# When ScalarE scales the blocks of w1 and w2: tied behind its own last cast, and queued after older blocks' casts

## The chip, the cores and the metric

The kernel runs on one core of a Trainium2 chip. The core has five engines that work side by side, each with a queue of its own in a fixed order: TensorE (PE in the profile), VectorE (DVE), ScalarE (ACT), GpSimd (POOL) and SyncE (SP), which here only issues transfers. The metric is the device time of one execution in microseconds, lower being better; times are compared as medians of several runs.

## The reference

```python
x = attention(q, k, v)            # B=4, H=8, S=576, D=64, causal window of 64 -> (2304, 512)
a = x @ w1; b = x @ w2            # 512 -> 1024 each
h = a * b @ w3                    # (a * b) @ w3, 1024 -> 1024
y = h @ w_out                     # 1024 -> 512
g = np.maximum(0.01 * (y @ w_in), y @ w_in)    # 512 -> 2048
out = g @ w_out2                  # 2048 -> 512
```

All weights arrive as float64 words, read as pairs of 32-bit integers.

## The kernel before

**Products.** Each fp32 product is made of three matmuls on operands split in a high and a low part (`mm3`, lines 77 to 79): high by high, high by low, low by high. The third one, line 79, is the first that needs the low part of the weights.

**Stages.** First the fold w3 @ w_out is computed (`w3_tr`, `w3_mm`, 16 steps), with the attention of the first 384 tokens between its steps. Then five chunks of tokens follow. A chunk has eight column steps f = 0 to 7: `ab_step(c, f, 0)` multiplies by w1, `ab_step(c, f, 1)` by w2, ScalarE and VectorE form their product and split it (lines 669 to 676), and `y_step` multiplies it by the fold. The `y_step` of f comes one step late, so that of f=0 stands after the products of f=1. A product's PSUM bank comes free when line 669 (first product) or line 674 (second) has read it; there are two such banks. Later stages (w_in, w_out2) follow and end the kernel.

**Conversion of weights.** Weights are converted from float64 in units. A unit is loaded by SyncE (`load_unit`, line 382), *scaled* by ScalarE with two activations (lines 417 and 391), *shifted* by VectorE (line 438), given its *sign* bits by VectorE (line 396), and *finished* by `store`: ScalarE casts the high part (line 332), and for w1 and w2 GpSimd subtracts to get the low part (line 333). `advance` moves up to four units on by one step each, and `until` calls it until a unit is finished.

**The eight units of w1 and w2.** They come last in this phase; here they are called B0 to B7: B0 is the first 256 columns of w1, B1 those of w2, B2 and B3 the next 256 columns of each, and so on. Steps f=0 and f=1 need B0 and B1, f=2 and f=3 need B2 and B3, and so on. B0, B2, B4, B6 share one place for raw words and one for the converted ones, B1, B3, B5, B7 the other. So the load of B2 can start when the sign step of B0 has read its words, and the shift of B2 can start when GpSimd has read the converted B0.

**What sets the order.** A scheduler decides where in each engine's queue an instruction stands, from priorities and its own estimate of times; the queue is then fixed. `tc.issue_after(x)` forces the instructions of a block to stand behind x on the same engine; it adds no wait on another engine. The first two units of w1 and w2 are loaded well ahead, during the fold; in the code, B0's scaling is written in the call `until(W12, PHASE_B)` after the fold's last step, and the scheduler moves it up.

Of the kernel before, what the change touches and what calls it, by code (L numbers as in the profile page):

```python
# [8 lines left out]
F32 = mybir.dt.float32  # L9
# [12 lines left out]
def tile_kernel(ctx: ExitStack, tc: tile.TileContext, q, k, v, w1, w2, w3, w_out, w_in, w_out2, out):  # L22
# [44 lines left out]
    act, dve, pool, pe, sp = nc.scalar, nc.vector, nc.gpsimd, nc.tensor, nc.sync  # L67

    def f32(ap):
        return ap.bitcast(F32)  # L70

    def first():

        return tc.high_priority(offset=3000)

    def mm3(ps, lh, ll, rh, rl, first, last, more=False):
        pe.matmul(ps, lhsT=lh, rhs=rh, start=first, stop=False, skip_group_check=more)  # L77
        pe.matmul(ps, lhsT=lh, rhs=rl, start=False, stop=False, skip_group_check=more)  # L78
        return pe.matmul(ps, lhsT=ll, rhs=rh, start=False, stop=last, skip_group_check=more).ins  # L79
# [243 lines left out]
    def cols2(t):  # L323
        return t.rearrange("p s (k m) -> p s k m", m=2 * P)
# [26 lines left out]
    def part_of(kind, dims, dt=F32):  # L351

        n = 1
        for d in dims:
            n *= d
        if words_in is not None:
            return words_in.tile([P] + list(dims), dt, name=kind, tag=kind, bufs=RAW)
        i = n_of[kind] % RAW
        n_of[kind] += 1
        x = {"raw": raw_all, "f": f_all}[kind][:, i].bitcast(dt)[:, 0:n]  # L360
        return shaped(x, dims)

    def feed():

        while n_of["load"] < n_of["cap"] and n_of["bits"] >= units[n_of["load"]]["after"]:
            load_unit()

    def load_unit():
        i = n_of["load"]
        u = units[i]  # L370
        n_of["load"] += 1
        u["raw"] = u["at"]() if u["at"] else part_of("raw", [UC], I64)
        with ExitStack() as how:
            if i >= PHASE_B:
                if i > PHASE_B + RAW:
                    how.enter_context(tc.issue_after(pss["store"]))
            else:
                how.enter_context(first())
            if "load" in pss:
                how.enter_context(tc.issue_after(pss["load"]))  # L380
            d = shaped(u["raw"], u["src"].shape[1:]) if len(u["src"].shape) == 3 else u["raw"]
            x = sp.dma_start(d, u["src"]).ins
        if i < PHASE_B:
            pss["load"] = x
            start_loads(i)
        else:
            pss.pop("load", None)

    def low_bits(raw, n=UC):

        act.activation(out=raw.bitcast(I32).rearrange("p (m two) -> p m two", two=2)[:, :, 0],
                       in_=raw.bitcast(U8).rearrange("p (m e) -> p m e", e=8)[:, :, 3],
                       func=AF.Copy, scale=1.0 / 32, bias=-31.0 / 64)

    def sign(f, hi):
        dve.scalar_tensor_tensor(out=f, in0=hi, scalar=-0x80000000, in1=f, op0=ALU.bitwise_and, op1=ALU.bitwise_or)

    def f_free(i):

        if i >= PHASE_B:  # L400
            return True
        a, n = units[i]["f_at"]
        for j in range(i):
            b, m = units[j]["f_at"]
            if a < b + m and b < a + n and (n_of["fin"] <= j or not units[j]["free"]()):
                return False
        return True

    def advance(stop):

        now = dict(n_of)
        if now["scale"] < min(stop, now["load"]):
            u = units[now["scale"]]
            w = u["raw"].bitcast(I32).rearrange("p (m two) -> p m two", two=2)
            u["lo"], u["hi"] = w[:, :, 0], w[:, :, 1]
            if now["scale"] < PHASE_B:
                act.mul(u["hi"].bitcast(F32), u["hi"].bitcast(F32), 2.0 ** -112)
                low_bits(u["raw"])
            else:
                u["f"] = part_of("f", [UC])  # L420
                with tc.issue_after(pss["copy"]):
                    act.mul(u["f"], u["hi"].bitcast(F32), 2.0 ** -112)
            n_of["scale"] += 1
        if now["fin"] < now["bits"]:
            u = units[now["fin"]]
            u["fin"](u["f"])
            n_of["fin"] += 1
        d = now["bits"] < now["shift"]
        if d:
            u = units[now["bits"]]  # L430
            f = u["f"].bitcast(I32)
            sign(f, u["hi"])
        if now["shift"] < now["scale"] and f_free(now["shift"]):
            u2 = units[now["shift"]]
            if now["shift"] < PHASE_B:
                i, n = u2["f_at"]
                u2["f"] = f_all[:, i:i + n].rearrange("p n m -> p (n m)")
                dve.scalar_tensor_tensor(out=u2["f"].bitcast(I32), in0=u2["hi"], scalar=3, in1=u2["lo"],
                                         op0=ALU.logical_shift_left, op1=ALU.bitwise_or)
            else:  # L440
                g = u2["f"].bitcast(I32)
                dve.tensor_scalar(g, g, 3, 0x7FFFFFF8, op0=ALU.logical_shift_left, op1=ALU.bitwise_and)
            n_of["shift"] += 1
        if d:
            if now["bits"] >= PHASE_B:
                dve.scalar_tensor_tensor(out=f, in0=u["lo"], scalar=29, in1=f, op0=ALU.logical_shift_right, op1=ALU.bitwise_or)
            n_of["bits"] += 1
            feed()

    def until(n, stop):  # L450
        while n_of["fin"] < n:
            was = dict(n_of)
            advance(stop)
            assert n_of != was
# [9 lines left out]
    pss = {}  # L464

    def w3_tr(f):
        t = p0.tile([P, 2, 4, P], F32R, name="w3T", tag="w3T", bufs=2)
        ps = ps_ab.tile([P, 4, P], F32, name="ab", tag="ab")
        for i in range(4):
            pe.transpose(ps[:, i, :], f[:, i], ident)  # L470
        both = t.rearrange("p s i k -> p s (i k)")
        act.copy(both[:, 0], ps.rearrange("p i k -> p (i k)"))
        pss["dve"] = dve.tensor_tensor(out=both[:, 1], in0=ps.rearrange("p i k -> p (i k)"), in1=f32(both[:, 0]),
                                       op=ALU.subtract).ins
        w3T.append(t)
# [48 lines left out]
    for gi in range(2):  # L524
        for l in range(2 if gi == 0 else 0, KF, 2):
            i = len(units)
            unit(w3[4 * P * gi:4 * P * gi + 4 * P, P * l:P * l + 2 * P].rearrange("(k p) m -> p k m", p=P), wide_w3(gi, l),
                 ("w3", gi, l), PLACES[i % 4], AFTER.get(i, i - 3), (2 * (i % 2), 2))
            if gi == 0:
                i = len(units)  # L530
                unit(w_out[P * l:P * l + 2 * P, :].rearrange("(k p) m -> p k m", p=P), store(("wo", l // 2), None),
                     ("wo", l), PLACES[i % 4], AFTER.get(i, i - 3), (2 * (i % 2), 2))
    W12 = len(units)
    for p in range(KD):
        for w, name in ((w1, "w1"), (w2, "w2")):
            i = len(units)
            unit(w[:, 2 * P * p:2 * P * p + 2 * P].rearrange("(k p) m -> p k m", p=P), store((name, p), None), (name, p),
                 PLACES[2 + i % 2], i - 3 if i < W12 + 2 else i - 1, (2 * (i % 2), 2))
    PHASE_B = len(units)
# [117 lines left out]
    def ab_step(c, f, j):  # L657
        n = W * CHUNKS[c][1]
        p, e = divmod(f, 2)
        ps = ps_ab.tile([P, 4, P], F32, name="ab", tag="ab").rearrange("p t k -> p (t k)")[:, 0:n]  # L660
        w = cols2(slots[("w1", "w2")[j], p])
        for kk in range(KD):
            x = xt[c, kk]
            ws = slice(P * e, P * e + P)
            pss["last"] = mm3(ps, w[:, 0, kk, ws], w[:, 1, kk, ws], x[:, 0, 0:n], x[:, 1, 0:n], kk == 0, kk == KD - 1)
        if j == 0:
            pss["a"] = gp.tile([P, CW], F32, name="a32", tag="a32", bufs=1)[:, 0:n]
            with first():
                pss["copy"] = act.copy(pss["a"], ps).ins
            return  # L670
        p32 = gp.tile([P, CW], F32, name="p32", tag="p32", bufs=1)[:, 0:n]
        t = gp.tile([P, 2, CW], F32R, name="ab", tag="ab", bufs=2)[:, :, 0:n]
        with first():
            dve.tensor_tensor(out=p32, in0=ps, in1=pss["a"], op=ALU.mult)  # L674
            act.copy(t[:, 0], p32)
            pss["dve"] = dve.tensor_tensor(out=t[:, 1], in0=p32, in1=f32(t[:, 0]), op=ALU.subtract).ins  # L676
        ab[f] = t

# [192 lines left out]
    for c in range(NC):  # L871
        for i in range(3 * KF):
            f, part = divmod(i, 3)
            if c == 0:
                if part == 0:
                    until(max(last[n, f // 2] for n in ("w1", "w2")), PHASE_B)
                if part < 2:
                    advance(PHASE_B)
            if part < 2 and (c == NC - 2 or c == NC - 1 and f):
                advance(KEPT)  # L880
            if c == NC - 1 and i in EARLY:
                early.pop(0)()
            if part < 2:
                ab_step(c, f, part)
            else:
                ysteps.append((c, f))
                if len(ysteps) > YLAG:
                    y_step(*ysteps.pop(0))
            slot()
# [341 lines left out]
```

## Time and profile before

| | us |
|---|---|
| median of 3 runs | 817.34 (816.06 to 817.37) |
| the profiled execution, its own time | 819.47 |
| its span, first to last instruction | 817.7 |
| TensorE busy in that span | 785.2 (96%) |

The profiled execution lies 2.13 us above the median, and 1.77 us of it lie outside the span. All times of instructions below count from the start of the span.

### The profile page before, as it was taken

Reading aid. Unit: us, or ns where it says so; the run is one execution under the profiler, and the core shown is the slowest. Engines: PE = TensorE matmul, PEld = TensorE weight load, DVE = VectorE, ACT = ScalarE, POOL = GpSimd, SP = SyncE. Lnnn points to the kernel's source line nnn. Section 1 sums busy time; section 2 is a strip of 40 time slices with the busy share of each in tenths; the row PEclk is TensorE's granted clock in tenths of the full one; section 3 lists DMA queues with packets and bytes.
Section 4 is the critical chain, followed back from the end, with each engine's and each line's share of the span. In section 5 each row is a group of like instructions: output and inputs, shape, how many; then the busy total and the mean of one; then the engine's idle time right before and its main releaser. Section 6 shows DMA issues by size and latency. Waiting matters only on the chain.

```text
span 817.7 us, 14546 instructions
## 1 busy us (share of the span) xinstructions
PE 785.2 (96%) x5128; PEld 724.6 (89%) x5128; DVE 572.2 (70%) x1349; ACT 431.7 (53%) x964; POOL 66.6 (8%) x61
## 2 busy tenths in 40 slices
PE   5879899999999999999999999999999999999997
PEld 4657699999988888888888899999999999999997
DVE  6995778457456546885731766867767999898976
ACT  6866675344334324443611655654556866575744
POOL 1022434112101100111000000000000000000000
PEclk9899999999999999999999999999999999999999
DMA  9995557347745556888420457998998754444321
GB/s 312 216 267 123 153 165 194 67 98 167 175 105 140 131 133 164 248 256 255 137 64 0 145 176 244 315 330 307 327 322 269 231 171 143 128 132 128 114 94 53
DMA packets 190809, 147.12 MB, mean 180 GB/s; under 512 B 124304, under 2 KB 150160, under 8 KB 190736
## 3 DMA queue, kind: packets, MB, share of 16 engines
q1 hardware_dynamic: 187712, 141.34, 59.1%
q10 hardware_dynamic: 3024, 4.85, 1.6%
q8 instruction: 40, 0.66, 0.3%
q14 instruction: 33, 0.27, 0.1%
HBM read 98.96 MB, written 47.19 MB: 179 GB/s over the span
## 4 chain that ended last, share of the span: by engine, by line
PE 78%; DMA 7%; SPq 5%; ACT 3%; DVE 2%; issue 1%; POOL 0%; ACTq 0%; DVEq 0%
PE ab L77 7%; PE o L78 7%; PE o L79 7%; PE ab L79 7%; PE ab L78 7%; PE o L77 7%; PE pr L77 6%; PE pr L79 6%; PE pr L78 6%; PE mm L78 4%; PE mm L77 4%; DMA raw<-in_moe_w_dram 4%; PE mm L79 3%; PE sc L245 3%; SPq L224 2%; SPq L623 2%
## 5 line engine op out<-in xcount | busy, mean ns | idle before, releaser
L79 PE MATMUL ab<-x,w 128*128 128x512 f32 (+1 forms) x320 | 119.9, 375 | 2.9 <-POOL w L333 2.9
L77 PE MATMUL ab<-x,w 128*128 128x512 f32 (+1 forms) x320 | 119.4, 376 | 2.0 <-ACT x L309 1.1
L78 PE MATMUL ab<-x,w 128*128 128x512 f32 (+1 forms) x320 | 119.9, 375 | 0.0
L77 PE MATMUL pr<-yop,w 128*128 128x384 f32 x300 | 101.5, 338 | 2.5 <-ACT c L826 2.5
L79 PE MATMUL pr<-yop,w 128*128 128x384 f32 x300 | 101.1, 337 | 0.0
L78 PE MATMUL pr<-yop,w 128*128 128x384 f32 x300 | 101.0, 337 | 0.0
L253 ACT ACTIVATE s<-s,nm 128x128 f32<-128x128 f32 x144 | 56.3, 393 | 47.5 <-DVE nm L249 47.5
L826 ACT COPY c<-pr 128x384 f32<-128x384 f32 x95 | 45.1, 479 | 66.2 <-PE pr L79 54.1
L78 PE MATMUL o<-yop,yop 128*128 128x256 f32 x259 | 73.1, 282 | 0.0
L79 PE MATMUL o<-yop,yop 128*128 128x256 f32 x259 | 73.0, 282 | 0.0
L77 PE MATMUL o<-yop,yop 128*128 128x256 f32 x259 | 73.0, 282 | 0.0
L79 PEld LDWEIGHTS ab<-x,w 128*128 128x128 f32 x320 | 60.5, 189 | 10.9 <-POOL w L333 3.2
L77 PEld LDWEIGHTS ab<-x,w 128*128 128x128 f32 x320 | 60.5, 189 | 10.8 <-ACT x L309 1.3
L78 PEld LDWEIGHTS ab<-x,w 128*128 128x128 f32 x320 | 60.6, 189 | 8.2 <-DVE x L310 0.3
L263 POOL TENSOR_TENSOR s<-s,rs 128x512 f32<-128x512 f32 (+1 forms) x40 | 42.4, 1062 | 291.0 <-DVE rs L262 213.1
L829 DVE TENSOR_TENSOR c<-pr,c 128x384 f32<-128x384 f32 x74 | 40.9, 554 | 31.0 <-PE pr L79 19.8
L674 DVE TENSOR_TENSOR p<-ab,a 128x512 f32<-128x512 f32 (+1 forms) x40 | 25.2, 631 | 52.3 <-PE ab L79 39.1
L968 ACT CAST yop<-raw 128x256 fp32r<-128x256 f32 (+1 forms) x92 | 42.4, 485 | 35.5 <-PE o L78 34.8
L78 PE MATMUL mm<-ab,wf 128*128 128x512 f32 (+1 forms) x160 | 59.7, 373 | 0.8 <-DVE ab L676 0.8
L77 PEld LDWEIGHTS pr<-yop,w 128*128 128x128 f32 x300 | 56.4, 188 | 3.8 <-ACT c L826 3.8
L79 PE MATMUL mm<-ab,wf 128*128 128x512 f32 (+1 forms) x160 | 59.3, 371 | 0.0
L77 PE MATMUL mm<-ab,wf 128*128 128x512 f32 (+1 forms) x160 | 56.5, 375 | 0.0
(137 smaller groups left out, 1956.9 us busy)
## 6 DMA issues: line engine op xcount, KB each, us to landing
hd<-c SPq DMA_DIRECT2D x96, 192.0 KB, 4.1
raw<-hd SPq DMA_DIRECT2D x32, 512.0 KB, 3.8
raw<-in_moe_w_dram SPq DMA_DIRECT2D x11, 1024.0 KB, 5.7
raw<-in_moe_w_out_dram SPq DMA_DIRECT2D x18, 512.0 KB, 5.3
raw<-in_moe_w_in_dram SPq DMA_DIRECT2D x16, 512.0 KB, 5.2
wd<-f SPq DMA_DIRECT2D x32, 256.0 KB, 4.1
raw<-wd SPq DMA_DIRECT2D x30, 256.0 KB, 4.4
pd<-tb SPq DMA_DIRECT2D x12, 512.0 KB, 3.0
```

The costliest lines, as they stand in the source:

```text
L77: pe.matmul(ps, lhsT=lh, rhs=rh, start=first, stop=False, skip_group_check=more)
L78: pe.matmul(ps, lhsT=lh, rhs=rl, start=False, stop=False, skip_group_check=more)
L79: return pe.matmul(ps, lhsT=ll, rhs=rh, start=False, stop=last, skip_group_check=more).ins
L224: sp.dma_start(dst, src)
L245: pe.matmul(sc[:, t, :], lhsT=qb[:, t, :], rhs=kT[n][:, k0:k0 + P], start=True, stop=True)
L253: act.activation(out=s[:, t, :], in_=s[:, t, :], func=AF.Exp, bias=nm[:, t:t + 1], scale=-1.0, accum_out=sm[:, t:t + 1])
L263: pool.tensor_tensor(out=s[:, 0:m], in0=s[:, 0:m], in1=rs[:, 0:m].unsqueeze(2).to_broadcast([P, m, P]), op=ALU.mult)
L623: pss["load"] = sp.dma_start(dst, src).ins
L674: dve.tensor_tensor(out=p32, in0=ps, in1=pss["a"], op=ALU.mult)
L826: pss["copy"] = act.copy(self.sb[to], ps).ins
L829: pss["add"] = dve.tensor_tensor(out=self.sb[to], in0=self.ps[at], in1=self.sb[of or to], op=ALU.add).ins
L968: tied("act", lambda: act.copy(out, x))
```

## The change

For the units of w1 and w2 alone, `advance` now calls the scaling at its end instead of its beginning, so that in the code it stands behind the finish and the bit steps of older units. And its two activations are tied by `issue_after` to the last cast that ScalarE made for the fold (`w3_tr`) or for a product of w1 and w2 (`ab_step`).

```diff
     def advance(stop):
 
         now = dict(n_of)
-        if now["scale"] < min(stop, now["load"]):
+
+        def scale_next():
             u = units[now["scale"]]
...
             if now["scale"] < PHASE_B:
-                act.mul(u["hi"].bitcast(F32), u["hi"].bitcast(F32), 2.0 ** -112)
-                low_bits(u["raw"])
+                with tc.issue_after(pss["act"]) if now["scale"] >= W12 else nullcontext():
+                    act.mul(u["hi"].bitcast(F32), u["hi"].bitcast(F32), 2.0 ** -112)
+                    low_bits(u["raw"])
...
             n_of["scale"] += 1
+
+        late = W12 <= now["scale"] < PHASE_B
+        more = now["scale"] < min(stop, now["load"])
+        if more and not late:
+            scale_next()
         if now["fin"] < now["bits"]:
...
             n_of["bits"] += 1
             feed()
+        if more and late:
+            scale_next()
...
-        act.copy(both[:, 0], ps.rearrange("p i k -> p (i k)"))
+        pss["act"] = act.copy(both[:, 0], ps.rearrange("p i k -> p (i k)")).ins
...
-            act.copy(t[:, 0], p32)
+            pss["act"] = act.copy(t[:, 0], p32).ins
```

The scheduler lays all queues out anew from this. The lines of the changed kernel are shifted by two to nine: 417 becomes 419, 438 becomes 445, 472 becomes 481, 493 becomes 502, 669 becomes 678, 674 becomes 683, 675 becomes 684.

ScalarE's queue at the end of the fold, before. `w3T_837` is the fold's last transposed block, `raw_98` the raw words of any unit (here of B2, then of B3), `w_104` to `w_107` are B0 to B3, `wf` the fold's result, `x` the attention output of the first chunk.

```order
L472 CAST w3T_837<-ab_838 128x512 [waits PE_49,Activation_49]
L417 ACTIVATE raw_98<-raw_98 128x1024 [waits DMAHW0_49]
L391 ACTIVATE raw_98<-raw_98 128x1024
L279 COPY pts_829<-ab_861 128x3x4x32 [waits PE_49]
L332 CAST w_105<-f_99 128x1024 [waits DVE_49]
L493 CAST wf_935<-mm_592 128x512 [waits PE_49]
L493 CAST wf_935<-mm_596 128x512 [waits PE_49]
L493 CAST wf_936<-mm_622 128x512 [waits PE_49]
L493 CAST wf_936<-mm_626 128x512 [waits PE_49]
L332 CAST w_106<-f_99 128x1024 [waits DVE_49]
L309 CAST x_905<-pa_892 128x384 [waits PE_49]
L417 ACTIVATE raw_98<-raw_98 128x1024 [waits DMAHW1_49]
```

The same place of the changed kernel, from the same cast on. The first pair of activations is now B0, the second B1.

```order
L481 CAST w3T_837<-ab_838 128x512 [waits PE_49]
L419 ACTIVATE raw_98<-raw_98 128x1024 [waits DMAHW6_49]
L391 ACTIVATE raw_98<-raw_98 128x1024
L419 ACTIVATE raw_98<-raw_98 128x1024 [waits DMAHW7_49]
L391 ACTIVATE raw_98<-raw_98 128x1024
L279 COPY pts_829<-ab_861 128x3x4x32 [waits PE_49]
L502 CAST wf_935<-mm_592 128x512 [waits PE_49]
L502 CAST wf_935<-mm_596 128x512 [waits PE_49]
L502 CAST wf_936<-mm_622 128x512 [waits PE_49]
L502 CAST wf_936<-mm_626 128x512 [waits PE_49]
L332 CAST w_104<-f_99 128x1024 [waits DVE_49]
L309 CAST x_905<-pa_892 128x384 [waits PE_49]
```

Before, the scaling of B0 stood behind the cast of the fold's tenth block and that of B1 behind the eleventh's, well above this piece; now both stand behind the cast of the sixteenth and last, and the cast of B0 behind the four casts of the fold's result.

What follows there in ScalarE's queue of the changed kernel: the three pairs of activations are B2, B3 and B4, `a32_988` is the first product of f=0, `ab_1012` the high part of the product of f=0.

```order
L419 ACTIVATE raw_98<-raw_98 128x1024 [waits DMAHW0_49,Activation_49]
L391 ACTIVATE raw_98<-raw_98 128x1024 [waits Activation_49]
L332 CAST w_105<-f_99 128x1024 [waits DVE_49]
L419 ACTIVATE raw_98<-raw_98 128x1024 [waits DMAHW1_49,Activation_49]
L391 ACTIVATE raw_98<-raw_98 128x1024 [waits Activation_49]
L279 COPY pts_1020<-pa_1016 128x3x4x32 [waits PE_49,Activation_49]
L332 CAST w_106<-f_99 128x1024 [waits DVE_49]
L678 COPY a32_988<-ab_975 128x384 [waits PE_49]
L419 ACTIVATE raw_98<-raw_98 128x1024 [waits DMAHW2_49,Activation_49]
L391 ACTIVATE raw_98<-raw_98 128x1024 [waits Activation_49]
L332 CAST w_107<-f_99 128x1024 [waits DVE_49]
L684 CAST ab_1012<-p32_1011 128x384 [waits DVE_49]
```

The cast of B1 (`w_105`) stands behind the scaling of B2, as it did before, and the cast of the product of f=0 (`ab_1012`) behind the scaling of B4 and the cast of B3; before, it stood behind the scaling of B4 and ahead of the cast of B3.

## Rows read from the trace of the kernel before

**Rows 1.** The page: each engine's busy time, share of the span, instructions.

```profile
PE 785.2 (96%) x5128; PEld 724.6 (89%) x5128; DVE 572.2 (70%) x1349; ACT 431.7 (53%) x964; POOL 66.6 (8%) x61
```

**Rows 2.** Windows: stretch, its length, busy time of each engine, granted clock, DMA.

```profile
60.00:90.00 30.00, 29.77 (x200) 24.20 (x198) 19.45 (x65) 20.49 (x55) 7.27 (x7) 0.93 0.49 120
90.00:106.00 16.00, 12.00 (x71) 9.88 (x70) 9.93 (x12) 10.14 (x15) 7.49 (x3) 0.89 0.62 197
106.00:134.00 28.00, 27.61 (x183) 26.80 (x183) 25.11 (x42) 19.02 (x36) 11.99 (x5) 1.00 0.65 180
134.00:160.00 26.00, 25.46 (x193) 24.68 (x194) 13.64 (x52) 11.82 (x39) 6.61 (x6) 1.00 0.49 112
160.00:813.00 653.00, 648.10 (x4288) 605.46 (x4287) 453.07 (x1081) 328.26 (x749) 26.52 (x24) 1.00 0.59 178
```

**Rows 3.** Timeline of PE, 93 to 111 us: start, duration, instruction, idle before.

```profile
93.71 1.07 PE L79 MATMUL mm<-w,w3T 128*128 128x512 f32 x4
94.62 0.33 PE L77 MATMUL ab<-x,w 128*128 128x384 f32 x1
...
97.99 0.44 PE L77 MATMUL ab<-x,w 128*128 128x384 f32 x1 [0.38 <-ACT w L332]
...
101.48 0.48 PE L79 MATMUL ab<-x,w 128*128 128x384 f32 x1 [2.87 <-POOL w L333]
...
105.59 0.34 PE L79 MATMUL ab<-x,w 128*128 128x384 f32 x1
106.17 0.44 PE L77 MATMUL ab<-x,w 128*128 128x384 f32 x1 [0.25 <-ACT a L669]
...
110.69 0.95 PE L77 MATMUL mm<-ab,wf 128*128 128x384 f32 x4
```

**Rows 4.** Timeline of ACT, 65 to 109 us.

```profile
65.06 1.13 ACT L417 ACTIVATE raw<-raw 128x1024 f32<-128x1024 f32 x1
...
68.59 1.14 ACT L391 ACTIVATE raw<-raw 128x1024 int32<-128x1024 uint8 x1
...
90.19 0.59 ACT L472 CAST w3T<-ab 128x512 fp32r<-128x512 f32 x1 [1.53 <-PE ab L470]
94.48 1.14 ACT L417 ACTIVATE raw<-raw 128x1024 f32<-128x1024 f32 x1 [3.70 <-DMA raw<-in_moe_w_dram]
95.51 1.13 ACT L391 ACTIVATE raw<-raw 128x1024 int32<-128x1024 uint8 x1
96.53 0.46 ACT L279 COPY pts<-ab 128x384 f32<-128x384 f32 x1
96.89 1.05 ACT L332 CAST w<-f 128x1024 fp32r<-128x1024 f32 x1
97.84 2.05 ACT L493 CAST wf<-mm 128x512 fp32r<-128x512 f32 x4
...
108.05 0.52 ACT L675 CAST ab<-p 128x384 fp32r<-128x384 f32 x1
```

**Rows 5.** Timeline of DVE, three bit steps of units B0, B1, B7.

```profile
83.00 1.22 DVE L438 SCALAR_TENSOR_TENSOR f<-raw 128x1024 int32<-128x1024 int32 x1
...
91.88 1.25 DVE L396 SCALAR_TENSOR_TENSOR f<-raw,f 128x1024 int32<-128x1024 int32 x1
...
130.45 3.31 DVE L396 SCALAR_TENSOR_TENSOR f<-raw,f 128x1024 int32<-128x1024 int32 x1
```

**Rows 6.** Timeline of POOL, low parts of B1 and B2, B6, B7.

```profile
98.02 5.77 POOL L333 TENSOR_TENSOR w<-f,w 128x1024 fp32r<-128x1024 f32 x2 [5.97 <-ACT w L332]
...
129.87 2.81 POOL L333 TENSOR_TENSOR w<-f,w 128x1024 fp32r<-128x1024 f32 x1 [4.57 <-PE sc L245]
...
135.13 2.38 POOL L333 TENSOR_TENSOR w<-f,w 128x1024 fp32r<-128x1024 f32 x1
```

**Rows 7.** Timeline of SP's queue: the load of B2.

```profile
88.91 0.38 SPq L382 DMA_DIRECT2D raw<-in_moe_w_dram  x1
```

**Rows 8.** DMA issues, 54 to 132 us: count, KB each, median us to landing.

```profile
raw<-in_moe_w_dram SPq DMA_DIRECT2D x8, 1024.0 KB, 5.5
```

## The prediction

> **What bounds the kernel now.** I read the page first: TensorE is busy for 785.2 of 817.7 us [rows 1], so a change elsewhere counts by what it adds to or takes from TensorE's idle time. Then the windows, to find where that idle time lies around the change [rows 2]. From 60 to 90 us, the second half of the fold, TensorE is idle for 0.23 us in 30; from 90 to 106 for 4.0 us in 16; from 106 to 134 for 0.4, from 134 to 160 for 0.5, and over the remaining 653 us for 4.9. So the only sizeable gap near the change is at the change from the fold to the first chunk. The timeline of TensorE shows what it waits for there [rows 3]: the fold's last matmuls start at 93.71, the first product of f=0 follows at 94.62, and the second product starts at 97.99 but stands at 101.48 for 2.87 us until GpSimd has made the low part of B1. f=0 ends at 105.93 (105.59 and 0.34), f=1 starts at 106.17, and the `y_step` of f=0 at 110.69.
>
> Why is B1 late? ScalarE's timeline tells it [rows 4]. It waits 3.70 us for the words of B2, scales them from 94.48, and only then, at 96.89, casts B1. The sign step of B1 had started at 91.88 and took 1.25, so B1 was ready at 93.1 [rows 5]: 3.8 us were lost because the cast stands behind a scaling that waits for a transfer. B0 has slack: its words were scaled at 65.06, shifted at 83.00.
>
> **The change part by part.** *What it removes.* Two scalings, 65.06 to 69.73 with one cast between them, 4 activations of about 1.05 us, leave ScalarE's queue in the fold [rows 4]. TensorE has only 0.23 us of idle time there [rows 2], so at most 0.2 us is gained; I take 0.
>
> *What it adds at the end of the fold.* I follow the new queues with the old durations. A scaling takes 2 x 1.03 = 2.06 us (94.48 to 95.51 is the first half) [rows 4], a shift or sign step 1.2 [rows 5], GpSimd's subtraction 2.38 alone and 3.4 beside VectorE (98.02 to 101.48; 5.77 for two) [rows 3, 6]. The load of B2 was issued at 88.91 and its scaling started at 94.48, so a load takes 5.57 [rows 4, 7]; the median of the eight is 5.5 [rows 8].
>
> 1. The fold's last cast ends at 90.8 (90.19 and 0.59) [rows 4]. B0 is scaled until 92.9, B1 until 94.9.
> 2. VectorE shifts and signs B0 from 92.9 to 95.3. Only now is the raw place free: the load of B2 is issued at 95.3, not 88.9, and B2 lands at 100.9.
> 3. ScalarE copies `pts` (0.36 from 96.53 to 96.89), makes the four casts of the fold's result, 1.9 to 2.05 [rows 4], and casts B0 until 98.3. GpSimd needs until 100.7 to 101.7. The first product of f=0, which ran at 94.62, gets past its third matmul at about 101.2.
> 4. ScalarE now stands before the scaling of B2, from 100.9 to 103.0, with the cast of B1 behind it, though B1 is ready at 99.4. The cast ends at 104.0, GpSimd at 106.4 to 107.6. Before, this wait ended at 101.48, so it ends 4.9 to 6.1 later.
> 5. Then ten matmuls of f=0 remain. At full clock 24 matmuls and three transposes took 4.5 (106.17 to 110.69), so ten take 1.8; just after the wait, 13 took 4.45 (101.48 to 105.93), so ten take up to 3.4 [rows 3]. f=0 ends at 108.2 to 111.0, against 105.93. With 4.5 for f=1 and its transposes TensorE would reach the `y_step` of f=0 at 112.7 to 115.5, against 110.69: 2.0 to 4.8 late.
> 6. What is late next is that `y_step` itself. Its first matmul needs `ab_1012`, which now stands behind the scaling of B4 and the cast of B3. B4 is loaded when the sign step of B2 is done. B2 is shifted from 103.0 to 104.1; if the sign step follows at once it ends at 105.3, B4 lands at 110.9, is scaled until 113.0, B3 is cast until 114.0 and `ab_1012` until 114.5. Before, `ab_1012` was cast at 108.05 [rows 4]. So TensorE resumes at 114.5 against 110.69, 3.8 late.
>
> *The unknown cost.* At 104.1 the sign step of B2 and GpSimd's subtraction of B1 start almost together. In the trace the sign step of B7 started at 130.45, while GpSimd subtracted B6 (129.87 to 132.68), and took 3.31, ending 1.1 after GpSimd [rows 5, 6]. If that happens to B2, its sign step ends at 106.4 + 1.2 = 107.6, 2.3 later, and step 6 gives 116.8: 6.1 late. If VectorE goes first instead, the subtraction ends at 107.6 and step 6 stays at 3.8, while step 5 gives at most 4.8. Both orders occur before (98.02 is the other), and the two are 0.1 us apart, so I take the middle: 5.0.
>
> The Trainium skill ("SBUF — State Buffer", section "SBUF: two separate sides") says that VectorE with two SBUF inputs and GpSimd share a port pair as an exclusive lock, and that whichever starts first holds it for the whole instruction. The rows of B7 agree with that. By the rule alone GpSimd, due at 104.0, goes first, and the sum is 6.1 rather than 5.0.
>
> *Later.* Behind step 6 the loads of B5 to B7 follow the same chain and are no later than B4's. An f takes 36 matmuls, some 6.7 us at 4.5 for 24, so f=4 comes 20 and f=6 some 33 us after the start of f=1; I find no further wait of over 0.5 us. Nothing gives the loss back: from there on TensorE is idle for 0.5 us in 26 and 4.9 in 653 [rows 2], and those waits hang on TensorE's own progress.
>
> *Sum.* -0 (fold) + 5.0 (one shift of everything behind 110.69, bounds 2.0 to 6.1) = 5.0. The profiled execution would go from 819.47 to 824.5 with a span of 822.7; against the median of 817.34 that is **822.3 us**.
>
> **The rivals.**
> - *Faster: ScalarE no longer stands before a scaling with a cast ready.* If the queue let the cast of B1 go ahead of the scaling of B2, B1 would be cast at 93.1 rather than 96.89, TensorE's wait would fall from 2.87 to nothing, and with the slow matmuls behind it 3 to 4 us would go: 813.6. For it: this wait is what the trace shows at 96.89. Against it: the new queue has the cast of B1 behind the scaling of B2 still, and B0's scaling cannot start before 90.8. It decides if B1 is cast before 96.9.
> - *No change: the late blocks are hidden.* 817.3. For it: B0 was no wait for the product at 94.62 [rows 3], and a load could land sooner than 5.57. Against it: B1 had none, and the way from the last cast to B1's subtraction holds 2 x 2.06 of scaling, 2.4 of bit steps and a load, 14 us, in place of the 10.7 from 90.8 to 101.48.
> - *Slower still: the waits for the shared steps add up.* If VectorE also stands behind GpSimd at the sign steps of B3 and B4, each adds up to 2.3 to the next load, and f=2 and f=4 wait too: 6.1 + 2.3 = 8.4, 825.7. For it: 3.31 at 130.45. Against it: before, such waits cost TensorE only the 0.5 us of 134 to 160.
> - *The change does nothing:* excluded, the scalings stand elsewhere in the queue.
>
> **How the numbers follow.** About 0.2%, 1.6 us, is what a measurement here can tell from no change. The forecast, 2.0 to 6.5 us slower, gets 0.62; slower still 0.18; no change 0.12; faster 0.08. So slower by over 0.2% is 0.80, within 0.12, faster 0.08. The range reaches from the edge of no change, 818.0, to the third rival with a margin, 826.8, and leaves out about 2 in 10.
>
> **What would show it.** In the new trace: the scaling of B0 directly behind the fold's last cast near 91; the load of B2 issued near 95; ScalarE idle from about 98.7 to 101 on that transfer; the cast of B1 near 103; TensorE idle twice, for about 6 us in all, between 95 and 108, and again briefly before the `y_step` of f=0 near 115; the same order of work and the same idle time after 140, moved by 5 us. The forecast is wrong if B1 is cast before 100, if the loads land within 3 us, or if the idle time after 140 falls by what was lost before.

## The result and the profile after

| | us |
|---|---|
| before, median of 4 runs | 816.7 (815.83 to 817.37) |
| changed, median of 4 runs | 826.84 (822.15 to 827.54) |
| ratio | 1.0113 [1.0073, 1.0152] |
| the profiled execution of the changed kernel, its own time | 822.15, span 820.4 |

The change makes the kernel slower, by 10.1 us. The forecast was 822.3 with a range up to 826.8, so the sign was right, and this median lies at the range's upper edge. The loss is about twice the forecast of 5.0 us. Two later medians of the same kernel were 825.13 and 826.92.

The profiled execution is the shortest of its four. By its page TensorE is busy for 1.1 us more than in [rows 1], in a span that is 2.7 us longer.

```profile
PE 786.3 (96%) x5128; PEld 724.5 (88%) x5128; DVE 575.4 (70%) x1349; ACT 432.5 (53%) x964; POOL 65.7 (8%) x61
```

The windows of the changed kernel, columns as in [rows 2]: stretch, length, busy time of PE, PEld, DVE, ACT, POOL, granted clock, DMA.

```profile
60.00:90.00 30.00, 30.00 (x210) 24.49 (x209) 16.38 (x56) 17.20 (x48) 5.74 (x7) 1.00 0.41 88
90.00:106.00 16.00, 10.75 (x50) 9.16 (x49) 13.69 (x13) 11.75 (x17) 7.41 (x3) 0.68 0.44 150
106.00:134.00 28.00, 23.99 (x157) 21.60 (x156) 24.76 (x39) 18.68 (x33) 12.89 (x6) 1.00 0.61 174
134.00:160.00 26.00, 26.00 (x197) 25.29 (x196) 11.79 (x51) 11.72 (x38) 6.44 (x6) 1.00 0.53 128
160.00:813.00 653.00, 648.61 (x4285) 606.09 (x4284) 453.94 (x1080) 328.73 (x750) 26.51 (x24) 1.00 0.59 179
```

From 90 to 160 us TensorE is idle for 5.25 + 4.01 = 9.3 us, against 4.9 before, and from 90 to 106 the granted clock is 0.68 against 0.89. Behind 160 the idle time is 4.4 us against 4.9. So the loss lies where the forecast put it, and nearly all of it stays.

The timeline of PE shows the waits, against [rows 3].

```profile
91.47 0.57 PE L306 MATMUL pa<-pts,x 128*64 128x64 f32 x12 [0.46 <-ACT pts L279]
...
94.35 0.69 PE L77 MATMUL ab<-x,w 128*128 128x384 f32 x1 [2.31 <-ACT w L332]
...
97.84 0.69 PE L79 MATMUL ab<-x,w 128*128 128x384 f32 x1 [2.48 <-POOL w L333]
...
108.57 0.45 PE L77 MATMUL ab<-x,w 128*128 128x384 f32 x1 [1.30 <-DVE p L683]
...
112.17 0.97 PE L77 MATMUL mm<-ab,wf 128*128 128x384 f32 x4 [0.92 <-ACT ab L684]
...
117.16 0.94 PE L245 MATMUL sc<-kT,qbd 128*128 128x128 f32 x6 [0.53 <-DVE qbd L236]
...
133.41 0.55 PE L276 MATMUL pa<-ident,s 128*128 128x128 f32 x3 [0.63 <-POOL s L263]
```

The first two long waits are for B0, its cast and its low part. Before, B0 cost nothing and the one long wait was for B1. The third is for a PSUM bank, which VectorE (line 683) frees late, and the fourth is the `y_step` of f=0. The timelines of ACT, DVE, POOL and SP give the reasons, against [rows 4 to 7].

```profile
86.34 0.59 ACT L481 CAST w3T<-ab 128x512 fp32r<-128x512 f32 x1 [1.05 <-PE ab L479]
86.82 1.17 ACT L419 ACTIVATE raw<-raw 128x1024 f32<-128x1024 f32 x1
...
88.89 1.15 ACT L419 ACTIVATE raw<-raw 128x1024 f32<-128x1024 f32 x1
...
93.23 1.07 ACT L332 CAST w<-f 128x1024 fp32r<-128x1024 f32 x1
...
96.60 1.12 ACT L419 ACTIVATE raw<-raw 128x1024 f32<-128x1024 f32 x1 [1.92 <-DMA raw<-in_moe_w_dram]
...
98.65 1.03 ACT L332 CAST w<-f 128x1024 fp32r<-128x1024 f32 x1
100.76 1.17 ACT L419 ACTIVATE raw<-raw 128x1024 f32<-128x1024 f32 x1 [1.08 <-DMA raw<-in_moe_w_dram]
...
108.64 1.12 ACT L419 ACTIVATE raw<-raw 128x1024 f32<-128x1024 f32 x1 [3.79 <-DMA raw<-in_moe_w_dram]
...
110.68 1.03 ACT L332 CAST w<-f 128x1024 fp32r<-128x1024 f32 x1
111.61 0.51 ACT L684 CAST ab<-p 128x384 fp32r<-128x384 f32 x1
```

```profile
94.35 1.22 DVE L396 SCALAR_TENSOR_TENSOR f<-raw,f 128x1024 int32<-128x1024 int32 x1
...
100.10 3.29 DVE L396 SCALAR_TENSOR_TENSOR f<-raw,f 128x1024 int32<-128x1024 int32 x1
...
104.57 3.48 DVE L396 SCALAR_TENSOR_TENSOR f<-raw,f 128x1024 int32<-128x1024 int32 x1
...
112.13 3.30 DVE L396 SCALAR_TENSOR_TENSOR f<-raw,f 128x1024 int32<-128x1024 int32 x1
```

```profile
94.37 3.41 POOL L333 TENSOR_TENSOR w<-f,w 128x1024 fp32r<-128x1024 f32 x1 [7.68 <-ACT w L332]
99.76 2.56 POOL L333 TENSOR_TENSOR w<-f,w 128x1024 fp32r<-128x1024 f32 x1 [1.98 <-ACT w L332]
104.56 2.40 POOL L333 TENSOR_TENSOR w<-f,w 128x1024 fp32r<-128x1024 f32 x1 [2.25 <-ACT w L332]
111.78 2.56 POOL L333 TENSOR_TENSOR w<-f,w 128x1024 fp32r<-128x1024 f32 x1 [4.82 <-ACT w L332]
```

```profile
91.56 0.39 SPq L382 DMA_DIRECT2D raw<-in_moe_w_dram  x1
...
103.47 0.37 SPq L382 DMA_DIRECT2D raw<-in_moe_w_dram  x1
...
108.12 0.37 SPq L382 DMA_DIRECT2D raw<-in_moe_w_dram  x1
```

ScalarE scales B0 and B1 behind the fold's last cast, so the load of B2 is issued late. ScalarE then stands before the scalings of B2, B3 and B4, 1.92, 1.08 and 3.79 us, each time for a load, and the casts behind them wait too. On VectorE the sign steps of B2, B3 and B4 (100.10, 104.57, 112.13) each stand beside a subtraction by GpSimd and take 3.3 to 3.5 us; that of B1 took 1.22. The loads of B4 and B5 (103.47 and 108.12) are issued 0.1 us behind the ends of the sign steps of B2 and B3 (103.39 and 108.05), so a longer sign step makes a later load.

**How executions are compared.** The fold's last cast (`w3T`) starts at 86.34 here and at 90.19 in [rows 4]. In two more profiled executions of the changed kernel, with the same queues, it starts at 91.42 and 85.36. When it starts varies by 6 us between executions, so times are counted from that cast: to the first matmul of the `y_step` of f=0, and to the copy (line 703; 694 before) that ends chunk 0. Both are read in each kernel's own timeline.

| kernel | cast starts | to the `y_step` | to the end of chunk 0 |
|---|---|---|---|
| before | 90.19 | 20.50 | 74.46 |
| changed, three executions | 86.34, 91.42, 85.36 | 25.83, 26.16, 26.03 | 81.32, 81.65, 81.57 |
| B0 and B1 alone changed | 87.90 | 25.99 | 81.47 |
| B2 to B7 alone changed | 86.72 | 20.16 | 74.14 |
| changed, B2 to B7 scaled behind casts | 87.99 | 23.02 | 75.83 |
| changed, low parts on VectorE, two executions | 85.97, 89.05 | 24.12, 24.07 | 76.58, 76.51 |
| B0 and B1 as before, B2 to B7 scaled behind casts | 88.63 | 14.86 | 68.52 |

Counted so, the loss is nearly the same in every execution: 5.3 to 5.7 us at the `y_step`, 6.9 to 7.2 at the end of chunk 0.

The windows from the cast to the `y_step`, before and then changed:

```profile
90.19:110.69 20.50, 16.33 (x98) 14.22 (x96) 13.85 (x17) 14.04 (x20) 8.58 (x4) 0.92 0.54 174
```

```profile
86.34:112.17 25.83, 18.36 (x97) 15.38 (x95) 19.14 (x17) 18.93 (x25) 9.11 (x5) 0.80 0.46 158
```

Of the 5.3 us, 3.3 are more idle time (7.47 against 4.17) and 2.0 are about the same matmuls at a lower granted clock. The clock does not set the end of this stretch: in the two later executions it is 0.87, and the stretch lasts as long, with more of it idle.

### The profile page after: what moved, and what is told of

It is laid out like the page before. It is cut to its first block, busy times and chain, and to the rows that moved or that the text cites. A ratio compares the mean times of both kernels' runs of the same rounds, so it can differ in the third digit from the quotient of the medians.

```text
span 820.4 us, 14550 instructions
## 1 busy us (share of the span) xinstructions
PE 786.3 (96%) x5128; PEld 724.5 (88%) x5128; DVE 575.4 (70%) x1349; ACT 432.5 (53%) x964; POOL 65.7 (8%) x61
## 4 chain that ended last, share of the span: by engine, by line
PE 83%; DMA 7%; ACT 4%; DVE 3%; SPq 2%; issue 1%; POOL 0%; ACTq 0%; DVEq 0%; POOLq 0%
PE o L79 7%; PE o L78 7%; PE o L77 7%; PE ab L77 7%; PE ab L78 7%; PE ab L79 7%; PE pr L77 7%; PE pr L79 7%; PE pr L78 7%; PE mm L77 5%; PE mm L78 4%; PE mm L79 4%; DMA raw<-in_moe_w_dram 3%; PE sc L245 3%; PE pa L306 2%; DVE f L396 1%
```

## The experiments

Ratios are to the kernel before, timed beside it on the same chip, with 95% intervals.

**The changed kernel again**, unaltered.

> The changed kernel once more, unaltered, since its runs lay 5 us apart (822.15 against 826.5 to 827.5) and its one trace is of the fastest. My theory (the blocks B0 and B1 are scaled behind the fold's last cast, so the load of B2 and the cast of B1 come late) gives the median 5 to 10 us above before, and in the trace again 5 to 6 us more from the fold's last cast to the y_step of f=0 than the 20.5 us of before. Rival: the distance between runs lies in the opening 60 us, whose queues are unchanged; then the wait that ended at 55.6 in the first trace ends 2 us or more later in a run of 827, and the stretch behind the last cast is unchanged.

Measured: 825.13 against 817.38, ratio 1.0092 [1.006, 1.0124]. The loss repeats. Of the 6.2 us between the spans of its profiled execution and of the first one (826.6 and 820.4), 5.1 lie ahead of the fold's last cast. So the rival is right on where these two differ, and the theory on the stretch behind the cast.

**Only B0 and B1 changed, and only B2 to B7 changed.** The first restricts the edit to the first two units, the second to the other six.

```diff
-                with tc.issue_after(pss["act"]) if now["scale"] >= W12 else nullcontext():
+                with tc.issue_after(pss["act"]) if W12 <= now["scale"] < W12 + 2 else nullcontext():
...
-        late = W12 <= now["scale"] < PHASE_B
+        late = W12 <= now["scale"] < W12 + 2
```

> Only B0 and B1 are scaled late and tied; B2 to B7 as before. My theory: these two carry the whole loss, 5 to 10 us slower than before and within 1 us of the changed kernel. Rival: the ties of B2 to B7 to the products' casts cost as well; then this one is slower by 2 us less than the changed kernel or better.

> Only B2 to B7 are scaled late and tied; B0 and B1 as before. My theory: within 1 us of before, with B1 cast behind the scaling of B2 and a TensorE wait of about 2.9 us there. Rival (the ties of B2 to B7 cost): 2 to 5 us slower than before.

Measured: 825.93, ratio 1.0095 [1.0069, 1.0121], for the first two; 816.17, ratio 1.0003 [0.998, 1.0026], for the rest. The two late units carry all of the loss. That B2 to B7 are tied and called late costs nothing by itself that shows here (interval -1.6 to 2.1 us).

**The rival "faster": the cast goes first.** B0 and B1 stay as before, and B2 to B7 are scaled only when the older units are cast.

```diff
-            act.copy(t[:, 0, sl], f)
+            pss["cast"] = act.copy(t[:, 0, sl], f).ins
...
-                with tc.issue_after(pss["act"]) if now["scale"] >= W12 else nullcontext():
+                with tc.issue_after(pss["cast"]) if now["scale"] >= W12 + 2 else nullcontext():
...
-        late = W12 <= now["scale"] < PHASE_B
+        late = W12 + 2 <= now["scale"] < PHASE_B
...
-        if more and late:
+        if more and late and n_of["fin"] >= now["scale"]:
```

> B0 and B1 scaled as before; the scaling of each later block is tied behind the cast of the block before it, so that the cast of B1 stands ahead of the scaling of B2. If ScalarE's standing before a scaling with a finished block behind it is what makes TensorE wait (my reading of both traces), the wait of 2.9 us for the low part of B1 goes and the kernel is 2 to 4 us faster than before. Rival: the low part of B1 is late for GpSimd's sake, or the later blocks now come too late; then 0 to 3 us slower than before.

Measured: 811.99 against 817.38, ratio 0.9925 [0.9899, 0.9951]: faster than both kernels, by 5.4 us against before and so by more than the 2 to 4 expected. Its window from 90 to 106 us holds 0.3 us of idle time where [rows 2] has 4.0, with a granted clock of 1.00 where that has 0.89:

```profile
90.00:106.00 16.00, 15.70 (x102) 14.13 (x99) 11.22 (x16) 11.05 (x17) 5.32 (x3) 1.00 0.54 190
```

So the wait of 2.87 us in [rows 3] was indeed the cast's place behind a scaling, and the changed kernel keeps that place.

**One of the two units late.** As the first of the pair above, with `now["scale"] == W12` for B0 alone, and `W12 + 1` for B1 alone.

> Only B0 is scaled late and tied; in the resulting queue B1 is scaled early and the casts of B0 and B1 both stand ahead of the scaling of B2. If the late start of the load of B2 (raw place freed late) is the larger part, the loss stays at 5 us or more against before. If the cast of B1 behind the scaling of B2, and the cast of f=0's product behind that of B4, are the larger part, 2 to 3 us are lost: B2 still lands near 101 on the clock of the trace of before, but B1's low part is done near 104 instead of 106.4 to 107.6, and the wait ahead of the y_step of f=0 goes.

> Only B1 is scaled late and tied; B0 as before. The queue now has the scaling of B2 ahead of the fold's last cast. If ScalarE simply stands before whatever is next in its queue, the fold's last cast waits for the words of B2 (it stood at 90.2 and these land near 94.5): TensorE waits 4 to 6 us inside the fold, B1 follows late as well, and the kernel is 6 to 10 us slower than before. Rival (the scheduler's place for the activations does not matter, since there is slack in the fold): within 2 us of before.

Measured against 815.89: B0 alone 818.68, ratio 1.0043 [1.0026, 1.0059]; B1 alone 822.37, ratio 1.0087 [1.0068, 1.0106]. So B0 alone loses 2.8 us, as its second reading (the places of the casts are the larger part) expected, and B1 alone 6.5, as its first. The scheduler orders other things too in each, so the two don't add up. With B0 alone, the timeline of PE has a wait of 2.28 us for its cast, then 0.33, and no wait for the low part, since other matmuls stand ahead of the first one that needs it:

```profile
94.68 0.44 PE L77 MATMUL ab<-x,w 128*128 128x384 f32 x1 [2.28 <-ACT w L332]
...
95.62 0.53 PE L77 MATMUL ab<-x,w 128*128 128x384 f32 x1 [0.33 <-ACT w L332]
```

With B1 alone, the scaling of B2 stands ahead of the fold's last cast, and the fold waits. ScalarE's timeline and then TensorE's:

```profile
91.30 1.10 ACT L419 ACTIVATE raw<-raw 128x1024 f32<-128x1024 f32 x1 [5.34 <-DMA raw<-in_moe_w_dram]
...
93.29 0.57 ACT L481 CAST w3T<-ab 128x512 fp32r<-128x512 f32 x1
```

```profile
93.91 0.80 PE L77 MATMUL mm<-w,w3T 128*128 128x512 f32 x1 [4.76 <-ACT w3T L481]
```

It is the same mechanism at another place: whatever stands behind a scaling waits for that scaling's load.

**No subtraction beside the sign steps.** VectorE makes the low parts of w1 and w2 in place of GpSimd, in the changed kernel and in the kernel with the cast first.

```diff
-            (pool if key[0] in ("w1", "w2") else dve).tensor_tensor(out=t[:, 1, sl], in0=f, in1=f32(t[:, 0, sl]),
+            dve.tensor_tensor(out=t[:, 1, sl], in0=f, in1=f32(t[:, 0, sl]),
```

> The changed kernel with the low parts of B0 to B7 subtracted by VectorE instead of GpSimd. If VectorE's sign steps of 3.3 to 3.5 us are waits for GpSimd's subtractions, they take 1.2 to 1.3 here; the subtractions then cost VectorE 1.85 each, so the time is within 2 us of the changed kernel, 6 to 9 us above before. Rival: the long steps have another cause (ScalarE, transfers), and stay at 3 us or more.

> The kernel with the casts ahead of the scalings (e4) and the low parts on VectorE. If what is left of the wait at the first products is GpSimd's 2.4 to 3.4 us against VectorE's 1.85, it is 0.5 to 2 us faster than e4, 805 to 812 us. Rival: VectorE, which also forms the products, becomes the one that is waited for; then 0 to 3 us slower than e4.

Measured against 815.89: the changed kernel with it 820.57, ratio 1.0072 [1.0051, 1.0092]; the cast-first kernel with it 810.08, ratio 0.994 [0.9919, 0.9962], not to be told from the cast-first kernel alone. The sign steps take 1.21 to 1.23 us, as expected, and the subtractions 1.2 (the last one 1.55) rather than 1.85. The first ratio leaves 5.9 us of loss (4.7 by the medians), less than the 6 to 9 expected. It overlaps with the ratios of the changed kernel, though its trace has 5 us less by the end of chunk 0. So it was timed again beside the changed kernel, below.

**B0 and B1 late, but no cast behind a waiting scaling.** The changed kernel with the cast-first rule for B2 to B7 only.

```diff
-                with tc.issue_after(pss["act"]) if now["scale"] >= W12 else nullcontext():
+                with tc.issue_after(pss["cast" if now["scale"] >= W12 + 2 else "act"]) if now["scale"] >= W12 else nullcontext():
...
-        if more and late:
+        if more and late and (now["scale"] < W12 + 2 or n_of["fin"] >= now["scale"]):
```

> B0 and B1 stay tied behind the fold's last cast, as in the change, but the scalings of B2 to B7 stand behind the casts of the two blocks ahead of them, so no cast waits behind a scaling that waits for a load. Theory (the change costs twice: B0 comes late for its first product, and from B1 on every load is late and every cast and copy behind the scaling is held): TensorE keeps the waits of about 2.3 and 2.5 us for the cast and the low part of B0, and the waits behind them (1.30 for the product, 0.92 for its high part, 0.5 and more in the later steps) go; idle 5.3 us against 3.9 of before, so 1 to 3 us slower than before, ratio 1.001 to 1.004. Rival (the two late blocks alone make the loss, however the casts stand): 6 to 8 us slower, ratio 1.007 to 1.010.

> The changed kernel unaltered, for comparison on one chip with the two others of this call. If the chip and the opening play no part: 7 to 8 us slower than before, ratio 1.009 to 1.010.

> The change with the low parts of w1 and w2 made by VectorE in place of GpSimd, timed beside the change itself. Theory (a sign step that stands beside GpSimd's subtraction takes 3.3 instead of 1.2 us and makes each next load later): 1.5 to 4 us below the change itself. Rival (the sign steps are hidden by ScalarE's wait for the loads): within 1 us of it.

Measured against 816.19: cast first 817.35, ratio 1.001 [0.9994, 1.0026]; the changed kernel 826.92, ratio 1.0118 [1.009, 1.0146]; low parts on VectorE 819.09, ratio 1.0036 [1.0016, 1.0056]. Beside this loss of 10.7 us, more than the 7 to 8 expected, the two edits take back 9.6 and 7.8 us by the medians, the second more than the 1.5 to 4 expected. The two timings of the low parts on VectorE differ (1.0072 and 1.0036, with intervals that just overlap), though their traces agree within 0.1 us up to the end of chunk 0. So how much that edit takes back is less certain than for the cast first.

The timeline of PE with the cast first keeps the waits for B0 and has none behind them up to the `y_step`:

```profile
93.13 0.57 PE L306 MATMUL pa<-pts,x 128*64 128x64 f32 x12 [0.46 <-ACT pts L279]
...
96.01 0.69 PE L77 MATMUL ab<-x,w 128*128 128x384 f32 x1 [2.31 <-ACT w L332]
...
99.50 0.69 PE L79 MATMUL ab<-x,w 128*128 128x384 f32 x1 [2.49 <-POOL w L333]
...
111.01 0.94 PE L77 MATMUL mm<-ab,wf 128*128 128x384 f32 x4
```

Its sign steps from B2 on no longer meet a subtraction either, so this edit does not part the two causes. Those of B2 and B3, in the timeline of DVE:

```profile
102.91 1.23 DVE L396 SCALAR_TENSOR_TENSOR f<-raw,f 128x1024 int32<-128x1024 int32 x1
...
110.47 1.23 DVE L396 SCALAR_TENSOR_TENSOR f<-raw,f 128x1024 int32<-128x1024 int32 x1
```

With the low parts on VectorE (the later execution), the timeline of PE has the two waits for B0, then two smaller ones, and none of 0.3 us or more from there to the end of chunk 0:

```profile
97.07 0.69 PE L77 MATMUL ab<-x,w 128*128 128x384 f32 x1 [2.29 <-ACT w L332]
...
100.10 0.69 PE L79 MATMUL ab<-x,w 128*128 128x384 f32 x1 [2.02 <-DVE w L333]
...
107.39 0.44 PE L77 MATMUL ab<-x,w 128*128 128x384 f32 x1 [1.28 <-ACT a L678]
...
113.12 0.97 PE L77 MATMUL mm<-ab,wf 128*128 128x384 f32 x4 [0.59 <-ACT ab L684]
```

Here the casts still stand behind the scalings, and the sign steps of B2 and B3, in the timeline of DVE, are short:

```profile
103.95 1.22 DVE L396 SCALAR_TENSOR_TENSOR f<-raw,f 128x1024 int32<-128x1024 int32 x1
...
106.94 1.23 DVE L396 SCALAR_TENSOR_TENSOR f<-raw,f 128x1024 int32<-128x1024 int32 x1
```

## Why the prediction was right, and where its size was off

**Steps 1 and 2 (B0 and B1 scaled behind the last cast, B2 loaded late): right.** Counted from that cast's start, the forecast was 0.6 and 2.7 us for the two scalings, 5.1 for the issue of B2's load and 10.7 for its scaling. The changed kernel has 0.48, 2.55, 5.22 and 10.26.

**Steps 3 and 4: right in the queue, wrong in the wait.** The cast of B1 stands behind the scaling of B2, and starts 12.3 us behind the last cast (12.8 forecast). But it was not what TensorE waited for. GpSimd had the low part of B1 by 102.3, and TensorE, held by B0 before and slowed by the clock behind it, needed it no earlier. In another execution that wait is 0.41 us. The waits for B0, 2.31 and 2.48, took its place. The prediction named as a sign of being wrong that B1 be cast before 100 us. It was, at 98.65; but this execution's fold ended 3.85 us earlier than the one before, and 12.3 us behind the last cast is 102.5 on the old count. The sign should have been counted from that cast.

**Step 6 (the `y_step` of f=0 is held by `ab_1012`, behind the scaling of B4 and the cast of B3): right, near its upper end.** The forecast gave 3.8 or 6.1 us and took 5.0; the three executions show 5.3 to 5.7. TensorE itself got there 4.4 us late in the first (5.3 less its wait of 0.92), within the 2.0 to 4.8 of step 5. GpSimd began the subtraction of B1 at 99.76, 0.34 us ahead of the sign step of B2, and the sign step ended 1.07 us behind it. So it was the order that cost more. The other order stands in the same trace: at 94.35 VectorE was 0.02 us ahead, kept its 1.22 us, and GpSimd took 3.41. The Trainium skill ("SBUF — State Buffer", section "SBUF: two separate sides") says that of GpSimd and VectorE with two SBUF inputs, whichever starts first keeps the shared port pair for its whole instruction. The trace agrees in both orders.

**The step that failed: "Later: I find no further wait of over 0.5 us".** The term for everything behind step 6 was put at nothing, and two costs are missing there.
- *Inside chunk 0.* The sign steps of B3 and B4 meet a subtraction as well. While that of B3 holds VectorE until 108.05, the product of line 683 stands behind it, and TensorE waits 1.30 us for its bank. This wait adds nothing to the 5.3 us at the `y_step`, which still waits 0.92 us when TensorE gets there. Behind that, waits of 0.53, 0.33 and 0.63 us follow, and by the end of chunk 0 another 1.5 us are lost. This is a part of the third rival, which put 2.3 us there.
- *At the start of chunk 1.* TensorE waits 1.51 us for `x` (line 309) in all executions of the changed kernel, against 1.11 before. In two of the four executions with B0 and B1 late and the queue otherwise unchanged, the granted clock falls behind that wait, and against the first execution each loses 1.5 to 1.6 us more within the next few matmuls. One of the two loses another 0.7 at 212.69, where it waits 1.80 us for a transfer and the first execution 1.12. The section on the hardware below shows the clock.

From the fold's last cast to the end of the span, the profiled execution before took 727.5 us. The four just named took 6.6 and 7.7 us more where the clock held, 9.0 and 10.4 where it fell. So the step at the `y_step` is 5.3 to 5.7 us, chunk 0 adds 1.5, and what follows adds -0.3 and 0.5 where the clock held, 2.0 and 3.3 where it fell. The medians say 7.7 to 10.7, in place of the sum of 5.0. How often the clock falls, and so where a median of four to six runs lies, was not counted.

**What made the loss.** It was not that B0 came late by itself. With B0 and B1 as late as in the change but the casts first, 1.2 us remain (interval -0.5 to 2.1, from the ratio's), and its trace has the waits for B0 unchanged. Nor was it the clock at the first products: over the 20 us from the fold's last cast the granted clock is 0.74 there, as in the changed kernel. The loss is a loop that B0's lateness starts: a sign step beside a subtraction takes 2.1 us longer, the next load starts as much later, ScalarE stands before that load's scaling, and the casts and product copies behind it come late. Two ways of cutting the loop were built. No work behind a waiting scaling (and, in the queue that results, no subtraction beside a sign step from B2 on) ends most of the loss. No subtraction beside the sign steps, with the casts left in place, ends a part: its two timings leave 5.9 and 2.9 us by their ratios. What each of the loop's links costs alone is not shown, since either cut also moves other work.

**The size, and luck.** The narrower forecast, 2.0 to 6.5 us slower, did not hold: the medians lie 7.7 to 10.7 above before. They lie around the rival "slower still" (8.4 us, chance 0.18). Its condition held in its first part, as the sign steps of B3 and B4 do stand behind GpSimd; but f=2 and f=4 did not wait for their weights. The range reached so far only because its upper end was drawn from that rival. Two of the three medians lie at that end or 0.1 us past it, so that it held is in part luck.

**The rivals.** "Faster" named the right lever: its own condition (the cast of B1 ahead of the scaling of B2) was built and gave 811.99, forecast 813.6; the change does not meet it. "No change" fell, as B0 had no slack left. (Its sum of 14 us is added wrongly: the terms that it names make 12.1, which is still more than 10.7.) The claim that nothing gives the loss back nearly held: from 160 us on, idle time is 4.4 us against 4.9.

## What to carry to other kernels

An engine with a fixed queue should not meet an instruction that waits for a load while work that TensorE needs soon stands behind it; put the short cast ahead, and read the gain from the wait of the engine that needs it. Before tying a step to a later point, follow what its result frees (here a place for the next load), because each load after it starts from there. Count times from an event ahead of the change when executions differ before it.

## What the runs showed of the hardware that was not expected

**The clock at the start of chunk 1.** Windows of the changed kernel, the execution read above and then a later one, each from 4 us behind the copy that ends chunk 0:

```profile
171.66:175.66 4.00, 3.59 (x22) 3.30 (x23) 2.11 (x11) 2.00 (x6) 0.00 (x0) 1.00 0.77 213
```

```profile
170.93:174.93 4.00, 3.59 (x14) 3.30 (x15) 1.11 (x2) 1.34 (x3) 0.00 (x0) 0.62 0.77 213
```

TensorE had the same queue ahead of both and waited 1.51 us in both, yet one goes on at full clock (2.4 GHz) and in the other the granted clock is 0.62 on average, between the levels of 1.2 and 2.4 GHz, with 14 matmuls done where the first did 22. Which execution it hits is not explained here.

**The stretch ahead of the fold's last cast** differs by 6 us (85.36 to 91.42) between executions of one kernel, about as much as the change costs at its place.
